# A one-core attention-and-MLP block on Trainium2: all engine queues in a newly found order, and a narrower marking product

## The chip, the core and the metric

The kernel runs on one core of one Trainium2 chip, in one launch. The core has five engines with a queue of instructions each: TensorE (PE; its weight loads are listed as PEld), VectorE (DVE), ScalarE (ACT), GpSimd (POOL) and SyncE (SP), whose queue here holds nearly all DMAs. 16 DMA engines move the data. The metric is the device time of one execution in microseconds (us).

## The reference

Two blocks on a sequence of 2048 tokens of width 512, in bf16. The first is linear attention with 32 heads of width 16, the second a gated MLP whose gate mixes the tokens with a 2048 x 2048 matrix.

```python
# A: x = A_x, 2048 x 512
q, k, v = heads(layernorm(x) @ wqkv)
phi = lambda t: where(t > 0, t + 1, exp(t)) + 1e-06
kv  = einsum('bhsd,bhse->bhde', phi(k), v)
z   = sum over tokens of phi(k)
o   = (phi(q) @ kv) / (phi(q) . z + 1e-06)
h   = x + o @ wo
# B
y   = gelu(layernorm(h) @ w_in)              # 2048 x 1792
z1, z2 = y[:, :896], layernorm(y[:, 896:])
g   = w_sp @ z2 + b_sp                       # tokens mixed, 2048 x 2048
out = h + (z1 * g) @ w_out
```

## The kernel before

**How it is recorded.** The kernel function records operations with an engine, a function that emits the instructions, the memory it reads and writes, and a cost (`_Prog.add`). Dependences follow from the memory. `schedule` takes the order of all operations from a packed string, `ORDER`; each engine's queue is that order cut down to the engine. `emit` writes the queues and puts a semaphore wait wherever a queue needs something of another engine or of a DMA. So the string decides what stands behind what on each engine, and nothing else of the order is decided at run time: an engine that waits holds up all that is queued behind it.

**Lines.** Every group of matrix products made by `matmuls` carries L434, every activation L453, plain DMAs L464 (`dma`), DMA transposes L467 (`dma_t`), and the sums and differences of `comb` L755. L815 are the DMAs that spread the reciprocals of the attention's denominators over the partitions (r, from rcp). L692 is the accumulation of the keys' outer products over the tokens.

**Stages.** Tokens are taken in 16 tiles of 128 (n = 0 to 15).

- Head: x arrives in pieces of one or two tiles. `k_unit(n)` handles the tiles n and n + 1: row statistics (VectorE, L543), reciprocal deviation (ScalarE or GpSimd), the normalized rows xn, their transpose xnT, the key product with wqkv, phi (L614, L619) into pk, and the accumulation L692. The first four tiles are transposed by TensorE (L602), all later ones by a DMA transpose on SyncE's queue:

```python
            if n < HEAD:                                        # HEAD = 4
                pe_transposes(xn[:, i, :], b + i % 2, xnT, i, second)
            else:
                g.last = dma_t(xnT[:, :, i * P:(i + 1) * P], xn[:, i, :], f"xt{i}")
```

- `q_unit` makes two 128-column chunks of the queries for 512 tokens; two units of the first 512 tokens stand among the first key tiles. Their weights are the DMA called wq.
- The loads of the weights that are needed later, w_v (a part of wqkv), wo, four halves of w_in (win1, win2) and the transposed blocks of w_sp (wt0 to wt15, two DMA transposes each), are recorded without a wait on any compute engine; that they follow the last load of x is the only order asked for. Where among the transposes of xnT they are issued is a matter of `ORDER`.
- Attention out: the value path (L790), denominators (L824), phi(q) times the reciprocals (L840), products with m, residual rows h (L852), and their normalized rows hn, transposed by DMA into hnT.
- MLP: Strassen-like cells (`cell3`, `cell2`, L882) form y with sums and differences of quarters of w_in (ws) and of hnT (hs); `mix` does the same for the product with w_sp, partly nested once more (`nested`, L1051), and applies the gate (L1030, L1031).
- Out: each gated tile z1 is transposed by DMA into zgT; `mo_pair` computes two output tiles from seven products in two PSUM banks X and Y (6 and 7, for the last pair 3 and 4), and `mo` the last two tiles. [...]

Of the kernel before, what the change touches and what calls it, by code (L numbers as in the profile page):

```python
# [32 lines left out]
class _Prog:  # L33
# [219 lines left out]
def bass_sequential_preLN__linear_attn_block__mixer_gmlp__prompt_kernel(  # L253
# [24 lines left out]
    g = _Prog(nc)  # L278
# [43 lines left out]
    x = g.sbuf("x", o_x, [NT, D], BF16)  # L322
    h = g.sbuf("h", o_x, [NT, D], BF16)
# [6 lines left out]
    hnT = g.sbuf("hnT", o_pk, [KD, S], BF16)  # L330
# [4 lines left out]
    z1 = [g.sbuf(f"z1t{n}", o_xnT + slot[n] * ZR, [FH], BF16) for n in range(NT)]  # L335
# [14 lines left out]
    N4 = HT // 2 * (HW // 2) * 2  # L350
# [65 lines left out]
    def bank(b, n=512, lo=0):  # L416
        return psum[:, b, lo:lo + n]
# [5 lines left out]
    def PE(fn, reads, writes, ns, **k):  # L423
        return g.add("PE", fn, reads, writes, cost=ns, lat=165, **k)
# [372 lines left out]
    for c in range(KD):  # L797
        b = CB[1 - c % 2]
# [18 lines left out]
    for tg in range(NG):  # L817
# [12 lines left out]
        if tg not in MERGE:  # L830
# [135 lines left out]
    lo, hi = slice(0, HW), slice(HW, FH)  # L966
# [227 lines left out]
    for k in range(0, HT, 2):  # L1194
# [5 lines left out]
        if k == 0:  # L1200
# [9 lines left out]
    PE(lambda pe: pe.matmul(bank(7), lhsT=hnT[:, 0, 0:P], rhs=wout[:, 0, :], start=True, stop=True), [hnT[:, 0, 0:P], wout[:, 0, :]],  # L1210
       [bank(7)], 216)
    wout_sums()
    for c, i in enumerate(MIX[:-1]):
        X, Y = (3, 4) if i == MIX[-2] else (6, 7)
        if Y != 7:
            rest, any_, w = psum[:, Y, HW:512], zgT[MIX[0]][:, 0, :], wout[:, 0, 0:512 - HW]
            PE(lambda pe, rest=rest, any_=any_, w=w: pe.matmul(rest, lhsT=any_, rhs=w, start=False, stop=True,
                                                               skip_group_check=True), [any_, w], [rest], 65)
        mo_pair(i, c % 2, X, Y)
# [34 lines left out]
```

## Time and profile before

| | |
|---|---|
| time, median of 3 runs | 224.73 us (223.61 to 225.98) |
| span of the profiled execution, first to last instruction | 222.3 us |
| the profiled execution's own time | not listed beside its span |
| busy: PE, DVE, ACT, POOL | 216.2, 202.8, 142.8, 47.1 us |
| matrix products and weight loads | 1346 each |
| granted TensorE clock | 1.000 |
| DMA | 27.12 MB, 57% of the 16 engines' time on SyncE's queue |

In the profile, a row of the timeline reads: start, duration (both us), engine, line, operation, output <- inputs, count; in square brackets the idle time before it and what ended it. A row of the windows reads: stretch, length, then busy time and number of instructions of PE, PEld, DVE, ACT and POOL, the granted clock, the share of the 16 DMA engines and GB/s. A row of the DMA view reads: what, queue, operation, count, size of one, median us from issue to landing. A row of the waits reads: engine, what it works on, line, what it waited for, total us, times, longest. "SPq" is SyncE's DMA queue.

### The profile page before, as it was taken

To read this page: it belongs to the slowest core of one execution; us is meant where nothing else is said; L and a number is where in the kernel's file an instruction comes from. 1 tells how busy PE (TensorE), PEld (TensorE's weight loads), DVE (VectorE), ACT (ScalarE), POOL (GpSimd) and SP (SyncE) were. 2 spreads that over 40 slices of the span, in tenths; PEclk is the share of its full clock that TensorE was granted. 3 is DMA by queue.
4 is the path that set the end of the run, shared out by engine and by line. 5 is a ranking of instruction groups with operands and counts; after the bars stand their busy time and mean duration, and the time that the engine had idled before them with its cause. 6 is when DMAs were issued, how large, how long until landed. Compare 5 with 4: busy or idle time off the path is not lost.

```text
span 222.3 us, 3865 instructions
## 1 busy us (share of the span) xinstructions
PE 216.2 (97%) x1346; PEld 123.6 (56%) x1346; DVE 202.8 (91%) x472; ACT 142.8 (64%) x283; POOL 47.1 (21%) x133
## 2 busy tenths in 40 slices
PE   7799999999999999999999999999999999999995
PEld 7443444443344444444555556666676787767764
DVE  3899967899999999999989998999999989899995
ACT  5789663299889999999872546626475246732330
POOL 4334410000547554685720000000000000000000
PEclk9999999999999999999999999999999999999999
DMA  6758877928966555304993653995372205033574
GB/s 182 246 99 227 170 180 181 237 50 193 182 137 132 112 107 85 49 0 94 179 134 88 166 116 81 161 202 107 58 152 58 41 0 70 17 88 27 127 203 142
DMA packets 75026, 27.12 MB, mean 122 GB/s; under 512 B 64768, under 2 KB 75008, under 8 KB 75008
## 3 DMA queue, kind: packets, MB, share of 16 engines
q1 hardware_dynamic: 74304, 26.30, 57.0%
q10 hardware_dynamic: 704, 0.59, 0.9%
q8 instruction: 10, 0.16, 0.3%
q14 instruction: 8, 0.07, 0.1%
HBM read 6.95 MB, written 2.10 MB: 41 GB/s over the span
## 4 chain that ended last, share of the span: by engine, by line
PE 87%; DVE 4%; DMA 3%; ACT 3%; SPq 1%; issue 1%; ACTq 0%
PE psum L434 79%; PE psum L692 6%; DMA x<-in_A_x_dram 1%; SPq L815 1%; DMA r<-rcp 1%; ACT e L453 1%; DVE pqT L840 1%; DVE h L852 1%; DVE st L543 1%; DVE pk L619 1%; PE psum L602 0%; PE psum L824 0%; PE psum L714 0%; PE psum L790 0%; DVE e L614 0%
## 5 line engine op out<-in xcount | busy, mean ns | idle before, releaser
L453 ACT ACTIVATE psum<-psum 128x448 f32<-128x448 f32 (+2 forms) x76 | 31.1, 428 | 34.9 <-PE psum L434 28.6
L434 PE MATMUL psum<-z,wt 128*128 128x448 bf16 (+1 forms) x216 | 42.0, 335 | 0.1
L434 PEld LDWEIGHTS psum<-z,wt 128*128 128x128 bf16 x216 | 20.9, 98 | 14.6 <-ACT np L453 0.4
L434 PE MATMUL psum<-win,hnT 128*128 128x448 bf16 x112 | 26.4, 353 | 0.0
L453 ACT ACTIVATE e<-psum 128x1024 bf16<-128x1024 f32 (+1 forms) x18 | 16.7, 929 | 8.5 <-PE psum L434 8.5
L453 ACT ACTIVATE z1t<-psum 128x448 bf16<-128x448 f32 (+1 forms) x24 | 16.4, 691 | 7.3 <-PE psum L434 5.3
L434 PE MATMUL psum<-ws,hs 128*128 128x448 bf16 x72 | 19.2, 353 | 0.0
L434 PEld LDWEIGHTS psum<-win,hnT 128*128 128x128 bf16 x112 | 10.5, 98 | 11.0 <-ACT z1t L453 1.0
L434 PE MATMUL psum<-zt,sa 128*128 128x448 bf16 (+1 forms) x92 | 16.5, 316 | 0.0
L882 DVE TENSOR_TENSOR psum<-psum,p5z 128x448 f32<-128x448 f32 x24 | 15.0, 626 | 1.0 <-ACT z1t L453 0.8
L692 PE MATMUL psum<-pk,xn 128*128 128x512 bf16 x64 | 15.8, 379 | 0.1
L453 ACT ACTIVATE p<-psum,b 128x448 f32<-128x448 f32 x22 | 13.4, 634 | 3.6 <-DVE u L1030 1.8
L434 PE MATMUL psum<-m,pqT 128*128 128x512 bf16 x64 | 14.7, 380 | 0.9 <-DVE h L852 0.6
L434 PE MATMUL psum<-xnT,wqkv 128*128 128x512 bf16 x64 | 15.3, 379 | 0.0
L453 ACT ACTIVATE z<-psum 128x896 bf16<-128x896 f32 x16 | 15.0, 970 | 0.2 <-PE psum L434 0.2
L434 PE MATMUL psum<-wqkv,xnT 128*128 128x512 bf16 x64 | 15.0, 379 | 0.0
L1030 DVE TENSOR_TENSOR u<-psum,p 128x448 bf16<-128x448 f32 x22 | 13.6, 620 | 1.4 <-PE psum L434 1.0
L434 PE MATMUL psum<-wout,zgT 128*128 128x256 bf16 (+1 forms) x77 | 14.9, 302 | 0.0
L434 PE MATMUL psum<-nv,nu 128*128 128x224 bf16 x108 | 14.5, 259 | 0.1
L543 DVE BATCH_NORM_STATS2 st<-x 128x6 f32<-128x512 bf16 x15 | 9.8, 682 | 3.6 <-DMA x<-in_A_x_dram 3.6
L614 DVE TENSOR_SCALAR e<-e 128x1024 bf16<-128x1024 bf16 (+1 forms) x18 | 7.0, 390 | 5.6 <-ACT e L453 5.6
L434 PEld LDWEIGHTS psum<-zt,sa 128*128 128x128 bf16 x92 | 8.9, 98 | 5.3
(157 smaller groups left out, 452.2 us busy)
## 6 DMA issues: line engine op xcount, KB each, us to landing
r<-rcp SPq DMA_DIRECT2D x16, 128.0 KB, 2.7
out_dram<-h SPq DMA_DIRECT2D x15, 128.0 KB, 1.8
win<-in_B_w_in_dram SPq DMA_DIRECT2D x4, 448.0 KB, 3.8
x<-in_A_x_dram SPq DMA_DIRECT2D x6, 256.0 KB, 3.8
wqkv<-in_A_wqkv_dram SPq DMA_DIRECT2D x2, 512.0 KB, 4.9
wout<-in_B_w_out_dram SPq DMA_DIRECT2D x1, 896.0 KB, 5.1
wt<-in_B_w_sp_dram SPq DMA_TRANSPOSE x32, 4.1
wo<-in_A_wo_dram SPq DMA_DIRECT2D x1, 512.0 KB, 6.4
```

Source lines behind the costliest of these rows:

```text
L434: inst = pe.matmul(out_ap, lhsT=a, rhs=b, start=start and i == 0, stop=stop and i == len(pairs) - 1, **kw)
L453: return g.add("ACT", lambda ac: ac.activation(out_ap, in_ap, func, **kw), [in_ap, *extra], [out_ap] + ([accum] if accum is not None else []),
L543: dve(lambda v: v.bn_stats(s[:, 0:6], src[:, n, :]), [src[:, n, :]], [s[:, 0:6]], D)
L614: dve(lambda v: v.tensor_scalar(e, e, 1.0, EPS_PHI, op0=ALU.min, op1=ALU.add), [e], [e], w * GW, acc=4)
L619: dve(lambda v: v.scalar_tensor_tensor(dst, t, 1.0 + EPS_PHI, e, op0=ALU.add, op1=ALU.max), [t, e], [dst], w * GW, ps=True)
L692: inst = pe.matmul(bank(CB[c]), lhsT=xn[:, i, c * P:(c + 1) * P], rhs=pk[:, i, :], start=i == 0, stop=i == NT - 1)
L815: g.add("SP", lambda q: q.dma_start(dst, src_ap), [rcp[:, i:i + w, :]], [dst], cost=700, lat=2200, dma=f"r{tg}{c // 2}")
L840: dve(lambda v, q=q, r=r: v.tensor_tensor(q, q, r, ALU.mult), [q, r], [q], 2 * GW, acc=2)
L852: dve(lambda v, n=n, b=b, s=s: v.scalar_tensor_tensor(h[:, n, :], bank(b), 1.0, x[:, n, :], op0=ALU.mult, op1=ALU.add, accum_out=s[:, 0:1] ...
L882: dve(lambda v: v.tensor_tensor(half(b), half(src), p, ALU.add), [half(src), p], [half(b)], HW, ps=True)
L1030: dve(lambda v: v.tensor_tensor(u, half(b), p, ALU.add), [half(b), p], [u], HW, ps=True)
```

## The change

The order string is another one, found by a new search over the same operations, and the product that marks bank 7 is made 64 columns wide, by the code that marked the last pair's bank:

```diff
-ORDER = "c-jrsg92EG76ibvyXVHXZM%(a+qN4!jcwbuZQHgR+kEdQX3Qd3M1#e%kQT`z..."
+ORDER = "c-jTQ0{|EY5Cp)zz5Up>8{4+i#<p#{v28WBZQHhO+v!Y101;q_2S*4Hkr4?(..."
...
-    PE(lambda pe: pe.matmul(bank(7), lhsT=hnT[:, 0, 0:P], rhs=wout[:, 0, :], start=True, stop=True), [hnT[:, 0, 0:P], wout[:, 0, :]],
-       [bank(7)], 216)
     wout_sums()
     for c, i in enumerate(MIX[:-1]):
         X, Y = (3, 4) if i == MIX[-2] else (6, 7)
-        if Y != 7:
+        if c == 0 or Y != 7:
             rest, any_, w = psum[:, Y, HW:512], zgT[MIX[0]][:, 0, :], wout[:, 0, 0:512 - HW]
             PE(lambda pe, rest=rest, any_=any_, w=w: pe.matmul(rest, lhsT=any_, rhs=w, start=False, stop=True,
                                                                skip_group_check=True), [any_, w], [rest], 65)
```

All five queues are in another order; the numbers of operations are the same (349 on TensorE, 456 on VectorE, 255 on ScalarE, 129 on GpSimd, 126 on SyncE). The first operations of SyncE's queue, before and after, with tiles in parentheses:

```
     before                            after
 1-4 x(0), x(2), wk, x(4,5)            the same
 5-8 x(6,7), x(8,9), wq, x(10,11)      the same
 9   xnT(5)                            x(12,13)
10   xnT(4)                            x(14,15)
11   x(12,13)                          wt10, second half
12   xnT(6)                            win2, first half
13   xnT(7)                            win2, second half
14   x(14,15)                          win1, one half
15   win2, first half                  wo
16   xnT(9)                            xnT(4)
17   xnT(8)                            xnT(5)
18   xnT(11)                           win1, other half
19   xnT(10)                           xnT(7)
20   win1, one half                    xnT(6)
21   xnT(12)                           xnT(9)
22   xnT(13)                           xnT(8)
...
33   wt10, one half                    wt0, one of ten wt blocks in a row
34   r (first of 16)                   wt11
43   r                                 r (first of 16)
```

TensorE's first twelve groups of four products after the transposes (K: key product of a tile; A: accumulation of a tile; Q: query product):

```
before  K0 K3 K1 K2 A0 Q Q Q A1 Q A2 K5
after   K0 K1 K2 K3 Q Q A0 Q Q A1 K4 K5
```

The accumulations A2 and A3 follow K5 in the changed order, then the key products of tiles 7 and 6. On VectorE the differences of w_in's quarters (ws) start seven places earlier, and more row statistics stand ahead of the normalization of tiles 4 and 5. The last products, the last additions and the last stores keep their order but for neighbours that change places.

More of the change, by code (lines that the diff above doesn't have):

```diff
@@ L15 @@
 SEM_NS = 45.0
-ORDER = "c-jrsg92EG76ibvyXVHXZM%(a+qN4!jcwbuZQHgR+kEdQX3Qd3M1#e%kQT`zTPO=_AuOClv8Wc>qFG!EZ()okbBk|*C9&w1z;at6OK3?grzN&zmdA2gDobv8EuW>f6jsPmS{lo5g)OZWup*Yu3R(=yVCgNU)v;n0%Q9Il%VHU=u4T5`*4FA-QLArREt|ErzpS`5vg}sU8e1D{XF05bwYPt)ft9urR?!+-U+Z8Ut&^3ps#ePSS!}Che_LlOYhA3rRkmvOuT`-D*3|}DIje3HZLl@9I5x<J*?7BQO>Brwvf)<4CRj}?Z<DQ=O|hXi&AM50n`$j=x^=giw#Zsq51VC6td%Xb#n#hi*fJYwy==LSuoZU8R@y4tWxZ{Wjk49Y+xA)?+h=QRwC%UqHpbT40Xt}iY>qv#n>N<w+F@H~M{J(WxAk_^#@PnjiUqdOHrY12ZCmY;J-3Cn-5%R9+hIHHxLvdBw%JbDe|FBE*-1NVr)-Ozw@bDS7wm<dw##<k&e#=uYCCb!Lg15qw2-)JpY4@>u$Xvfp+LN}SO7vJ3}WMp3Gt8!@$uCnBQfH@5g;ypSQ31*DEMwE@Y7NwIieyV{#a7{vT!g&M>0f1SUj)<_-!$e2Dy<6X;Bt=5FQzj5=D>>c@Y8WQ32%;5&4i2`B4-FP#*Uz5(=UYilHL1pg0PlKI$SX3Zn!{A~RYe8%iM)D&cRmLj%;qU#N^WsDhqoh#aVjYAB5@$d2}Cgg&T_GU$cjXpDc*7i}>LwU7(7(E*2%6JOB;M=$~%u?zpA6Q-dlYM?WEV>G&8CTe0oMq)aeVJXI77VcO-%)kot$1)7SYz#zm9K~2HM|XTf3yi}`%)ubs!vTE99lW<5IDxr1hOYR5L%5HY=!U!aiIZ4`*Y*&<&<dxp8jmm@$1wp1@c<KX8bk3IZ|oAD;1vdA9<uW?hG0I<U=3bl0j^*Ya_}mK;WyS|3f^EH{@^b<jc2hP<Tb3vTf`^$H?KoHhpC9mw-zuY6YvHWBPZi=GD7h`B;p2y<~xL7E+*zvB;<K4#506p628YG+(cwPM{agwQbu7KZo~&vR#--5ccx`DF2N>*V>;$xU0y(5_F#TS=VlaSc&6t?^yCY~U?F})ZD!yt6ksprV;z1%M%H5y-bQ^UV^KC>VP;})He@j-XJ+<cITmLGenulkWK8bhOEhMAreG_^;=kO^5{%8(tiUYn%bkqGHXO(=NXd%a#Z=77ww%jK?9Y-M#5gR)*&M)j+|4=c$0i)Y_8iQiT)=ru&G~G~1Kh)5T*%UF#&OKX;cU)D+=2Hj!?#?_@m$5qoWOUyYsdKyS92meup^i716%N+P2vcyVM~7GWPavueBwwRW)&{wT2^H>e&Ifh;uNmqRDS1Zp5QW0<5za#L9XXse&ZOP<PR?A3ZCKyj^!`@<VKd|5pLpdPUj)6<Z13_bwZo@hi7>1|Mc#~3{stWlr<;?a^2^7hR_y<)Ha@FD0Sg6&SYp^WIEkr6@^hvhSeor;8xycI9=v7hSw}U;uTicRX$)Ob!7xS=0ir*9$aT+)#43C(Gx~fRNdr%jIO7wqpFIfTa2M+yv>-Zr8|tRnu?>i+Q)h-sCatLgo>}6ddURJr9{fB#LB0nN}?C6uU9OpWGbeHdd&t(uHt&bluDu8YNQfMrIJdoLQ11js;wf*q|$1v!b+|3%C9CWqY65q?5e9uYN`Tip|V=4f0R)zl}ByVUagf?9aK)u)LE0&T$xovUDQ!iv|Jg~Nz>KVE2^t{sG7QIn!2l%dTN0F)=IVWHJYJp8mND~zxrvWX6d`;Xtidmx7KQ|)~THasjYr!yf$dC)@!5s=!k}>msaVh7HX(QsDp3PFm2W%4Od?s)>ci`NS)Nb+M;Eer)?Ug(ORN|`b+bbR^j}VCTN$&=(iT=tj21wj%%DIYP$|;w|1zL?^O=%R7XFppW3HCdaN_bqU##zdlcT!>4yH(Bpp*EKd)4NNf&feceFy6wO<!?Kv(tT|7G72{H}f}vR~12MfENo-DCPa(L1}my}wX2cfY2mx~*9LQh~?u2;S9WdmF#6DBjIOcz5sN!#%Et^amQ@J$=6S@)#b<M|p3L=lQ*lztX?n*ZX^X590$pu@CZop2QRQ0w3V1J)w{GAwI^3`Wub)<UZcVc`^^}6aAqkcqxCRbUw+`dm_){lf9}Z^(p>LQ$3@<)oV@nus+Rac?zH5GrfS%@wvX;7y4p<r$xTR)A)NW^_0Hcmw5*Ntd;&jJAH+x^~}D?cX%d0?`yr9XYtj3!6SMO&*|$utFQ4*UfTciY@Xe7d39gs1%0D$@W1_|F8Xf&q%FS3w|XJZ>wA5$@Aopk&$sz5Kj?-1fS2_zI^>r;pFi`XUe1quO+V#_{iN6OuR7wFy|$P4V_wH|`w6e$SG<PT^D}<d>v|C{=JoxB7xk<D+^_j{Z|uXoxZm^!-o#6K3BTbDy`nesTi)Coc?<uh+kV$8`5nLSoBf_w_A1`gANfOn;30yR{@7pnYiBUqTm3)skiiq5=W&AnJXD~dwZHK&LFnL}hYQ~NX%8C&!3Pf?y!3Pa-aUvE#0{SMM~@Ih3E~A2gD)OE_~y}qPyWLr2Qh-r9yR#s@q?JbFOL;`^#noe;JYUZ{&>RRw<iuPND}-H1t^N4"
@@ new lines @@
+ORDER = "c-jTQ0{|EY5Cp)zz5Up>8{4+i#<p#{v28WBZQHhO+v!Y101;q_2S*4Hkr4?(fT)OqxQK@MNP=95j-*I{JV=N{NQT@<jJ)^@`H&LHksqm$0)>$pF;D<SkOnbP5JgcNX%P$QQ4{G98->sc84w2<Q42e*4Kkw`G9fG4A`6P64z8m$N+28RA|$fo2I`>{%Ht+Vq73??9j>7Q+T(B3M?>U519U)XghEIBgNmqverSX)sD!Hc7yVHg1CSH9Fc8(y730wuq0tG|5e5@55lt`{oiPZ*5EhFO4rS34lTZVbF&yPE1w+sb-7yu-F%;7<9o;Y!3o!#N&;yIG1iP^mEwK!bF$+C063fvG;qeG7FaoRb6#roq_FyO0pf`45C7xg}_F*)(SRahRe$2)JtinNz#T*>MI2^`YJjXgb#5}CU3mm}~tjBy@#RhD}M%=~%Y{MQqitRXt9oTN0a2$7V7F+EEHsd7j;|$(mo1MZroW=v3$3<MgCw#yT3u&Km2_F%{F5@n);2C1tON27oJ;bumW){X`+ZVXSvsXxD@l6)lz9O;3wZMKLiN&#Rh+^N7+<xL0{<5f+$`aZigtKG@i*89RnuWCl_8X}!hUKyFmePt^UQ1*DSOm*w8LXH^wDOkU(pw5EU}deKrL)>r+zMGFOKat<gcY{TR?;e15i4c&EQ^)4I@ZdvS|+P#Ijp|5wYpZxGFo=4Y@6+nwYDmj(|TG}YiHT4nl-RK*2@mtaI0zUt*_OxHa5!2SZ@2*I@nkH+d5h<>uuHTnDw&}HqH854eMm1ZKTb#&eqVT+ZgL&OKhLbutqk^j#y(`YRj#O{bvL0fDN=|_RaQNQ(Iw2?YND#@7CS!+Bj=rw{5l^w3XJ<=GaebW^?U?-LdiZ!|vI8tg;?9$X?@t{j!s`+8)|{n`h1Kl&!Hhcw}qsqII=(_Sjz8Q0r!wEE^}-X`64a?XnHF?3`#<?6(cEw-9sija@Zzk`1%B7N3hOC#RV6k6p8=7BDVDG6BI{G{$2nKC#7?h}Z3%-LTL+W4W1_A^6lLTS7jwjds?;FbUt=O^eJAmYR8(l$-3MMPWCdv-K91QJIF_xxk|FmWAU&E5zrPm**`ld$5uh;3tdDI^1CC*pvDB!t${o`>+-ZbFal<QPyP<re|&TVlgJ;1*^~E?91N#i!oW24VawuSc3mD1sgIJGjKa&^QARnIfmypMqo*1WE@6hOMbTU%)}jR#evMsNSwn8Y|SrLiYd91ZCILF*q>!sk%Raj2e2)7aW?yLE{Cuk=d&?~avt|F6$f)Sn{XHxuqnr}J^$u#X5~WevbXHOMSRbW9M6^9&q{2@34F(6tjrHw#VVZ0s_ewYY|at<$VvRn)tt;v9LYmm!@XR>Q5?-F{KBam!xsF?<6O#rIE~-Amfv`Q%lL!KxsJcMp4E7m8~B?mxRD1roj<vWe>j%rn+ZS5t)w4eb#~@Go?|tiLHE-PTz-^ic!DAP4nz8RUSL`e?Ohql?{W*n_)LcNaNdO%8Qu%|Dc0ag)?@^~#D~1fh<=%~c%N4o$*=JdBl~q$@!B56A2XUq^#{DcCyee-S<@?f43FhCJf=V6O~&?Hyv?{C$DgyV$Mb~#g7H0<zhnZ>>iIm8=l8_EhXp;UC-K}~%wMsdC-dU|n)UrJZ{VHuh9$g%Qh0LD;|;x}r}R>u!Bcx-FYUFwsHgKrUdD@fIZx#U{BLjU<^8zV@r?eDH}Q(T#G8A2&+F;EthexX-r6g8Ca>;Iy@R*%$==L6`&8d;Exn7c@V1`AtNLp1=xe=)cT`u;=H0xt*83FS;5~i1Z}K*p;cdLXck)@@PTjqqukiu?-E;af@8!eQ+q3vUAE8m2>EnH{ANK#ej}P)8KF$035&zd$`fOk7BYci$_n|(_H~Ime>%)DEkMw!Iz|;6D-|U(FgpcyAzR*YeQD5voe7+y^Q@+l(`62)52YtIw@G*YU$NCQ6>EnE&FY>lJ?aTd)k5oAA_Ot%m!|R-1^j&`5JL`|{^$Y&kFZmvy<kvis_W5Oh<WKy%N0ABI@6i=ixBZGg_ZuEfH=T;9ryfhG)kV*|y<B&^t6q3F#Zh<l&|UAPm)=wNe4ctMf?`Yh<ptD7|0<>WDo_md*L;OgTrE^T4N^S4@&OvC*B)P?6jGx#RAV$mi4|I7b=AWti4y3Rk5^v3@q|jIM2f7xG*S0`oRTV)Cg_2ORa(9EhdxQ^G*$0>x~gchX6e1}&=f6D1|`>L&!w4~rqcT0GqgyvwOA1~M+LP+DYR7ElwQlULff@mUp$jm>YOrar`G7BXVxmE(I;Q0^IEMe+Mw*(sH|G6Y+A1z+NI6ftt~2}+}fkPDx`~grkvWR!pf)o`di=pfQo3p{?T(C)K{;n>N=vbI;3MdtQtC@nmVbYDyLdHrQ<59+Pb9EDz7?vsk%C&%etU?s;1)Fsw>K)s~W6p+N4G*p&Kfu>uRi0DyjOapr&e|v%0BfYN+PArHZ<v+q$PFs;pspAPes5q5e~dpoLy(u3oF9?u)?_g$xwL2`VX6@K_$a(Nl#E!UU}pE_kc3!8?6W5QGoj>xCXEZV)N>s0hIq#S0<^-xMYIsmMXJAZqYQ(S!KG4}DgQAXX4F_^Mw@5PVmn;ExgpzZE-393V&%{12myilG"
```

## The prediction

> **What bounds the kernel now.** I read the page of the profiled execution first, for the busy shares, and then its windows stretch by stretch.
>
> ```profile
> span 222.3 us, 3865 instructions
> ...
> PE 216.2 (97%) x1346; PEld 123.6 (56%) x1346; DVE 202.8 (91%) x472; ACT 142.8 (64%) x283; POOL 47.1 (21%) x133
> ```
>
> ```profile
> 7.96:16.59 8.63, 8.63 (x43) 3.85 (x41) 8.00 (x24) 7.05 (x12) 2.67 (x8) 1.00 0.67 156
> 16.59:23.95 7.36, 7.24 (x33) 2.95 (x32) 6.98 (x14) 5.95 (x7) 2.70 (x8) 1.00 0.92 217
> 23.95:45.90 21.95, 21.95 (x117) 9.48 (x115) 17.25 (x28) 10.85 (x15) 2.90 (x8) 1.00 0.83 191
> 45.90:54.40 8.50, 8.37 (x57) 3.78 (x57) 8.04 (x14) 8.13 (x12) 0.00 (x0) 1.00 0.45 103
> 54.40:67.70 13.30, 12.46 (x59) 5.06 (x60) 12.44 (x33) 11.56 (x26) 6.24 (x21) 1.00 0.77 158
> 67.70:171.90 104.20, 103.98 (x615) 58.08 (x616) 101.06 (x232) 75.06 (x156) 28.81 (x70) 1.00 0.59 110
> 171.90:219.50 47.60, 47.60 (x370) 35.21 (x367) 44.27 (x123) 19.75 (x50) 0.00 (x0) 1.00 0.35 76
> ```
>
> A row gives the stretch, its length, the busy time of TensorE, its weight loads, VectorE, ScalarE and GpSimd, the granted clock, the share of the 16 DMA engines and GB/s. TensorE is the bound from 7.96 us to 219.5 us at full clock. Its idle time is 0.12 us in the second stretch, 0.13, 0.84 and 0.22 us in the fourth to the sixth, and none in the others: 1.3 us in all. (A product's record is 379 ns and its slot 216 ns, as four take 0.86 us below, so a wait under 0.16 us doesn't show here; with some ten such waits the truth may be near 3 us.) So reordering can win little, and a wait that an order adds on TensorE before 219 us goes into the time nearly whole.
>
> The head is where the orders differ most, so I read the timeline of TensorE there, and that of SyncE's DMA queue.
>
> ```profile
> 7.96 3.62 PE L434 MATMUL psum<-wqkv,xnT 128*128 128x512 bf16 x16
> 11.41 1.03 PE L692 MATMUL psum<-pk,xn 128*128 128x512 bf16 x4
> 12.28 2.75 PE L434 MATMUL psum<-xnT,wqkv 128*128 128x512 bf16 x12
> 14.87 1.03 PE L692 MATMUL psum<-pk,xn 128*128 128x512 bf16 x4
> 15.73 1.03 PE L434 MATMUL psum<-xnT,wqkv 128*128 128x512 bf16 x4
> 16.59 1.03 PE L692 MATMUL psum<-pk,xn 128*128 128x512 bf16 x4
> 17.46 1.89 PE L434 MATMUL psum<-wqkv,xnT 128*128 128x512 bf16 x8
> ```
>
> ```profile
> 7.52 0.47 SPq L464 DMA_DIRECT2D wqkv<-in_A_wqkv_dram  x1
> 8.04 0.51 SPq L464 DMA_DIRECT2D x<-in_A_x_dram  x1
> 11.88 3.27 SPq L467 DMA_TRANSPOSE xnT<-xn  x2
> 15.20 0.58 SPq L464 DMA_DIRECT2D x<-in_A_x_dram  x1
> ```
>
> From 7.96 to 16.59 us TensorE does ten groups of four products of 0.863 us each on the first four token tiles. The group at 17.46 us is the first on tiles 4 and 5, whose normalized rows come through the DMA transposes issued at 11.88 and 13.2 us. SyncE issues them with nothing new queued in between after the load at 8.04 us.
>
> **The change, the wide product.** The marking product is taken out and a narrow one put in.
>
> ```profile
> 176.12 0.21 PE psum L1210
> ...
> 212.07 0.03 PE psum L1217
> ```
>
> In the chain that ended last the 512-column product is worth 0.21 us, the existing 64-column one 0.03 us. I take 0.18 us gained. It can't be more than 0.21; below, it is nothing if TensorE waits there for the transposed gate tile, which the products beside it read as well.
>
> **The change, the early SyncE queue.** After the load that stands at 8.04 us, the changed order issues, before the first transpose: the last two loads of x (256 KB each), half of a transposed block of w_sp (256 KB), three of the four loads of w_in (448 KB each) and w_o (512 KB). Before, only the transposes followed. By issue time alone this costs nothing: six loads of 0.47 to 0.58 us and one weight transpose, 1.39 us in the row below, end near 13.2 us, and VectorE now normalizes tiles 4 and 5 later too (its queue has more row statistics ahead of them, so near 13.5 us). The price is in the data. How the queue lands what it is given is seen where the kernel before puts two loads ahead of a transpose (issue times from the timeline, times to landing from the DMA views of the stretches around each issue):
>
> ```profile
> 37.22 0.58 SPq L464 DMA_DIRECT2D wqkv<-in_A_wqkv_dram  x1
> 37.84 0.51 SPq L464 DMA_DIRECT2D wo<-in_A_wo_dram  x1
> 38.39 5.60 SPq L467 DMA_TRANSPOSE wt<-in_B_w_sp_dram  x2
> ...
> 53.77 1.39 SPq L467 DMA_TRANSPOSE wt<-in_B_w_sp_dram  x1
> ```
>
> ```profile
> wqkv<-in_A_wqkv_dram SPq DMA_DIRECT2D x1, 512.0 KB, 5.2
> wo<-in_A_wo_dram SPq DMA_DIRECT2D x1, 512.0 KB, 6.4
> ```
>
> ```profile
> wt<-in_B_w_sp_dram SPq DMA_TRANSPOSE x1, 6.7
> ```
>
> Landings are 42.4, 44.2 and, for the transpose issued at 38.39, 45.1 us: in the order of issue, 1.8 us apart for 512 KB (284 KB per us), and 0.9 us for the transposed 256 KB. With little ahead of them transposes of xnT need half as long:
>
> ```profile
> xnT<-xn SPq DMA_TRANSPOSE x12, 3.2
> ```
>
> So the transpose of tile 4 will land behind everything issued earlier. The queue's state at the point where the orders part is known:
>
> ```profile
> wqkv<-in_A_wqkv_dram SPq DMA_DIRECT2D x1, 512.0 KB, 4.6
> x<-in_A_x_dram SPq DMA_DIRECT2D x1, 256.0 KB, 4.7
> ```
>
> These are the issues at 7.52 and 8.04 us; they land at 12.1 and 12.7 us. Ahead of tile 4 there are then 2 x 256 + 256 + 3 x 448 + 512 = 2624 KB. At 284 KB per us that is 9.2 us; with 0.45 us for its own 128 KB (half of 0.9) it lands at 12.7 + 9.2 + 0.45 = 22.4 us. The bounds are the fastest and a slow stretch of the DMA engines here:
>
> ```profile
> 40.00:42.00 2.00, 2.00 (x19) 0.79 (x21) 1.29 (x3) 1.13 (x2) 0.00 (x0) 1.00 1.01 352
> ```
>
> 352 GB/s (344 KB per us) gives 7.6 us and a landing at 20.8 us; the 217 GB/s at a share of 0.92 in the stretch 16.59:23.95 is 230 KB per us at a full share, 11.4 us and 24.6 us. I take 22.4, since its rate comes from loads of these very shapes with a backlog. [...]
>
> In the changed order TensorE's first ten groups are the same ten as before in another sequence; the eleventh and twelfth are tiles 4 and 5, ahead of the two accumulations that stood at 16.59 and 19.18 us. TensorE reaches the query products at 11.4 us and waits 0.7 us for their weights (landing 12.1), so it stands before tile 4 at 17.3 us, in order, with everything else queued behind it, and stays there until 22.45 us. Against 16.59 us that is **+5.9 us** (4.2 to 8.0). The queue behind follows: tile 5 lands 0.45 us after tile 4; one more w_in load (1.6 us) and two transposes bring tiles 6 and 7 to near 25.4 us, and TensorE wants them after four groups, at 25.9 us.
>
> **What comes back.** (a) The eight groups from 16.59 us take 7.36 us before but only 8 x 0.863 = 6.91 us of work; their waits were for a tile's exponent and product, which the four groups between now cover: -0.45 us. (b) VectorE and the loads are ahead by then: w_in is there early, and the differences of its quarters stand earlier in VectorE's queue.
>
> ```profile
> L755 DVE TENSOR_TENSOR ws<-win 128x896 bf16<-128x896 bf16 x4 | 2.4, 608 | 0.0
> ```
>
> Four of these, and those made from them, can run in the hole. In front of the first residual row VectorE has the same instructions in both orders, and 5 us more time for them. Of the 1.2 us idle from 45.9 to 171.9 us I take 0.9 as won back; the ends are 2.2 (all, with short waits that the records hide) and 0, since these waits are loops from TensorE over ScalarE, DMA and VectorE back to TensorE, and such a loop keeps its length wherever it starts. (c) The product, -0.18. Later queues are rearranged locally, gate and weight transposes by a few places; I cost them at nothing, since TensorE waits for no DMA but those of the head:
>
> ```profile
> PEld psum L434 <- DMA xnT<-xn: 0.6, 2, 0.4
> ...
> PEld psum L434 <- DMA wqkv<-in_A_wqkv_dram: 0.2, 1, 0.2
> ```
>
> What hides the later ones is that they land ahead of their use; if that cover is gone, one such place costs up to a landing, 3 to 4 us. The tail (last stores, last products) keeps its order.
>
> Sum: 5.9 - 0.45 - 0.9 - 0.18 = **+4.4 us**. The span is 222.3, so 226.7; around the span lie about 2.4 us (median 224.73 less span, as the profiled execution's own time isn't shown beside it), which gives **229.1 us**. With the ends: 4.2 - 0.45 - 2.2 - 0.2 = +1.4 (226.1) and 8.0 - 0.45 = +7.5 (232.2).
>
> **Rivals.** *Transposes get past the loads* (not slower): the queue spreads each DMA over 16 engines, and if a transpose lands as its 3.2 us says (issue near 13.5, landing near 17), TensorE waits 0.7 us for the query weights and nothing more. Then 222.3 + 0.7 - 0.45 - 0.9 - 0.18 = 221.5, time 223.9. It decides as soon as tile 4 lands before 17.4 us. For it: the transpose issued right behind a w_in load near 19.5 us took only 3.8 us.
>
> ```profile
> xnT<-xn SPq DMA_TRANSPOSE x1, 3.8
> ```
>
> Against: wo and the weight transposes at 6.4 and 6.7 us. [...]
>
> *The wait is there, but most is given back*: fast DMA (+4.2) and all of the later idle time, 226.1 to 226.6 us. For it: 1.3 us of visible idle; against: no idle at all from 23.95 to 45.9 and from 171.9 on.
>
> *SyncE itself is held up*: two weight transposes behind 1 MB took 5.60 us to issue, not 2.8. If tile 4's issue ends only as w_o lands (21.5 us), tile 5 follows 1.25 us later and lands near 24.8 (+1.4), and ten weight transposes at 1.39 us, which now stand ahead of the r round, reach it 1 to 2 us late: 4.4 + 1.4 + 1.2 = +7.0 us, 231.7.
>
> **How the numbers follow.** Forecast (wait of about 6 us, little returned) 0.70; overtaking 0.10; mostly returned 0.10; queue held up 0.10. The range 225.8 to 232.0 holds the forecast's bounds and most of the second and third; outside lie the first and some of the last, under 0.2. A measurement of this kernel tells about 1% (222.5 to 227.0) from no change. Faster by over 1% needs overtaking and more idle time won than the records show: 0.04. Within 1%: the rest of the first and two thirds of the second, 0.13. Slower: 0.83.
>
> **What would show it.** In the profile after: TensorE idle for about 5 us from 17.3 us, released by the DMA of xnT; the longest landing of xnT near 9 us; DMA share near 1 from 12 to 22 us; the following stages like before, about 4 to 5 us late; the last products 5 us later with the same tail. If xnT lands within 4 us and TensorE doesn't stop at tile 4, the mechanism is wrong; if it stops for 5 us and the time still rises by under 2 us, the term that failed is what comes back.

## The result, and the profile after

The changed kernel takes 235.22 us (median of 4 runs, 233.22 to 235.58) against 224.7 us: a ratio of 1.046, 95% interval 1.040 to 1.052. It is slower, as forecast, but by 10.5 us where 4.4 were forecast, and beyond the range of 225.8 to 232.0. The profiled execution took 235.17 us with a span of 233.4, 11.1 us more than before.

The page of the kernel after, and its windows over the stretches that the prediction showed of before:

```profile
span 233.4 us, 3850 instructions
...
PE 218.3 (94%) x1333; PEld 123.5 (53%) x1346; DVE 203.7 (87%) x472; ACT 143.0 (61%) x283; POOL 50.9 (22%) x133
...
PEclk9999799999999999999999999999999999999999
```

```profile
7.96:16.59 8.63, 7.72 (x36) 3.36 (x36) 8.30 (x24) 6.01 (x10) 3.31 (x10) 1.00 0.95 264
16.59:23.95 7.36, 1.78 (x7) 0.57 (x6) 4.12 (x8) 2.46 (x3) 3.69 (x11) 0.91 1.23 289
23.95:45.90 21.95, 21.84 (x96) 9.70 (x97) 14.55 (x24) 11.66 (x14) 3.50 (x9) 0.95 0.57 125
45.90:54.40 8.50, 8.45 (x54) 3.32 (x52) 6.24 (x10) 4.72 (x8) 0.00 (x0) 1.00 1.05 169
54.40:67.70 13.30, 11.58 (x69) 5.13 (x68) 11.51 (x22) 11.18 (x19) 1.47 (x3) 1.00 0.88 185
67.70:180.90 113.20, 111.51 (x645) 60.15 (x646) 108.89 (x253) 81.76 (x171) 36.25 (x87) 1.00 0.48 93
180.90:230.50 49.60, 48.71 (x371) 35.48 (x374) 45.82 (x123) 20.44 (x51) 0.00 (x0) 1.00 0.35 72
```

From 16.59 to 23.95 us TensorE was busy for 7.24 us before and for 1.78 us now. The granted clock, 1.00 in every stretch before, is 0.91 and 0.95 in two stretches here. And idle time stands where there was hardly any: 1.7 us in the stretch from 54.4, 1.7 in the next and 0.9 in the last, against 0.84, 0.22 and 0.00 in the corresponding stretches before. (The last two stretches end 9 and 11 us later than those of before, to hold about the same work.)

TensorE's timeline of the kernel after:

```profile
12.27 1.89 PE L434 MATMUL psum<-xnT,wqkv 128*128 128x512 bf16 x8 [0.83 <-DMA wqkv<-in_A_wqkv_dram]
...
23.18 3.31 PE L434 MATMUL psum<-wqkv,xnT 128*128 128x512 bf16 x8 [5.58 <-DMA xnT<-xn]
26.32 1.89 PE L692 MATMUL psum<-pk,xn 128*128 128x512 bf16 x7
...
63.44 4.48 PE L434 MATMUL psum<-m,pqT 128*128 128x512 bf16 x20 [1.56 <-ACT e L453]
...
150.16 0.56 PE L434 MATMUL psum<-z,wt 128*128 128x224 bf16 x4 [0.54 <-ACT z1t L453]
...
222.95 0.50 PE L434 MATMUL psum<-vs,us 128*128 128x256 bf16 x3 [0.58 <-DVE us L755]
```

The first two rows are the head as forecast: the wait for the query weights, then the stop at tile 4. The last three are waits of the later stages. The row at 23.18 holds one more thing: its eight products take 3.31 us, where eight such products take 1.89 us at 12.27.

To see where the time is lost I compared the kernels at equal work: I added up the slots of TensorE's products in queue order (0.216 us for 512 columns, less in proportion: 0.190 for 448, as eight of those take 1.68 us at 173.35 us of the kernel before, with a record of 0.352 us) and noted by how much later than before each kernel starts the product at which the sum has reached a given value. (Some of these traces lack the records of 12 or 13 products; they are counted in at their weight loads, which are all there. The products that e5 adds are left out.) The times in the first column are those of the kernel before; of the seven kernels behind "after" each is described at its experiment.

```
 before   after  e2     e3     e5     e6     e7     e9     e10
  16.2    +0.7   +0.1   +0.3   +0.5   +0.6   +0.3   +0.6   +0.2
  26.5    +7.5   +5.8   +2.0   +5.3   +6.9   +1.6   +2.1   +0.6
  51.6    +7.6   +8.5   +2.0   +5.4   +6.9   +1.7   +2.2   +0.6
  57.2    +9.0   +8.9   +7.0   +6.7   +6.9   +1.7   +2.2   +0.6
  88.4    +8.9  +10.2   +5.9   +7.0   +7.1   +1.6   +2.0   -0.1
 137.0    +9.1  +10.1   +6.1   +7.7   +7.3   +1.8   +2.0    0.0
 143.6    +9.9  +10.5   +6.7   +8.3   +8.4   +2.6   +2.0   +1.1
 161.6   +10.3  +10.5   +6.6   +9.3   +8.3   +2.7   +2.0   +1.0
 209.7   +10.4  +15.4   +6.6   +9.5   +8.3   +2.9   +1.8   +0.9
 216.0   +11.0  +15.6   +7.1   +9.6   +8.4   +3.7   +1.8   +1.3
```

Column "after" has three steps: 7.5 us in the head, 1.5 us near 57 us (the products that need phi(q) times r), and 1.9 us from 137 us on. No step leads back.

### The profile page after: what moved, and what is told of

Read it like the earlier page. It is cut to its first block, busy times and chain, and to the rows that moved or that the text cites. A ratio compares the mean times of both kernels' runs of the same rounds, so it can differ in the third digit from the quotient of the medians.

```text
span 233.4 us, 3850 instructions
## 1 busy us (share of the span) xinstructions
PE 218.3 (94%) x1333; PEld 123.5 (53%) x1346; DVE 203.7 (87%) x472; ACT 143.0 (61%) x283; POOL 50.9 (22%) x133
## 4 chain that ended last, share of the span: by engine, by line
PE 68%; DVE 15%; DMA 12%; POOL 1%; issue 1%; ACT 1%; SPq 1%; DVEq 0%
PE psum L434 61%; PE psum L692 5%; DMA zgT<-z1t 5%; DMA xnT<-xn 4%; DMA x<-in_A_x_dram 3%; DVE nv L755 2%; DVE u L1030 2%; DVE pqT L840 1%; DMA r<-rcp 1%; DVE st L543 1%; DVE nu L755 1%; DVE h L1188 1%; DVE h L852 1%; SPq L464 1%; DVE wt L755 1%
## 5 line engine op out<-in xcount | busy, mean ns | idle before, releaser
L453 ACT ACTIVATE psum<-psum 128x224 f32<-128x224 f32 (+2 forms) x76 | 31.3, 425 | 34.6 <-PE psum L434 27.1
L434 PE MATMUL psum<-wqkv,xnT 128*128 128x512 bf16 x63 | 16.2, 405 | 5.7 <-DMA xnT<-xn 5.6
L434 PE MATMUL psum<-ws,hs 128*128 128x448 bf16 x72 | 18.7, 353 | 0.0
L453 ACT ACTIVATE p<-psum,b 128x448 f32<-128x448 f32 x22 | 13.4, 633 | 5.6 <-PE psum L434 2.3
L434 PEld LDWEIGHTS psum<-win,hnT 128*128 128x128 bf16 x112 | 10.6, 98 | 10.9 <-ACT z L453 0.9
L434 PEld LDWEIGHTS psum<-wqkv,xnT 128*128 128x128 bf16 x64 | 6.4, 103 | 14.1 <-issue 7.7
L567 POOL TENSOR_SCALAR st<-st 128x1 f32<-128x1 f32 x10 | 4.8, 481 | 37.6 <-ACT sh L453 33.0
```

Source lines behind the costliest of these rows:

```text
L434: inst = pe.matmul(out_ap, lhsT=a, rhs=b, start=start and i == 0, stop=stop and i == len(pairs) - 1, **kw)
L453: return g.add("ACT", lambda ac: ac.activation(out_ap, in_ap, func, **kw), [in_ap, *extra], [out_ap] + ([accum] if accum is not None else []),
L567: pool(lambda p: p.tensor_scalar(s[:, 2:3], s[:, 0:1], s[:, 0:1], -1.0 / (n * n), op0=ALU.mult, op1=ALU.mult), [s[:, 0:1]], [s[:, 2:3]], 240)
```

## The experiments

Two theories stood against each other. **The queue**: the loss comes from the order of SyncE's queue, by the backlog of loads ahead of xnT, by the slow clock behind the wait, and by the weight transposes ahead of the r round. **The orders**: the changed orders of the other engines cost a good part by themselves. The kernels differ in queue orders alone, except for e4 and e5 and for the narrow product, which e2 and e10 have too. The runs of one kernel differ by 0.5 to 4.3 us here, so a difference of 1 to 3 us between two kernels is read together with the traces.

**e1 and e2: the queue alone, one way and the other.** e1 is the kernel after with SyncE's queue of before. e2 is the kernel before with SyncE's queue of after:

```diff
 e1:  TensorE, VectorE, ScalarE, GpSimd: as after
-     SyncE: as after
+     SyncE: as before
 e2:  TensorE, VectorE, ScalarE, GpSimd: as before
-     SyncE: as before
+     SyncE: as after
```

> The changed kernel with one queue exchanged: SyncE issues its DMAs in the order of the kernel before; TensorE, VectorE, ScalarE and GpSimd keep the changed orders, the product stays narrow. Theory Q (the loss of 10.5 us comes from SyncE's queue alone: the backlog in front of xnT, the slower clock behind the wait, the weight transposes ahead of r): 223 to 226 us, xnT landing within 4 us, no wait of TensorE over 1 us. Theory O (the other engines' orders cost a good part too): 228 us or more with the xnT wait gone.

> The kernel before with only SyncE's queue in the changed order (all other engines in the order of before; the product narrow). Theory Q: 233 to 237 us, TensorE idle about 5 to 6 us in front of the first tile that comes through a DMA transpose. Theory O: 229 to 231 us, the rest of the loss being the other engines'.

e1 took 254.91 us (ratio 1.134, 1.126 to 1.142), and its waits for xnT were not gone (three, 3.2 us in all). e2 took 240.55 us (1.076, 1.069 to 1.082), above the ranges of both theories. Both are slower than either kernel, which neither theory expected. Rows of TensorE's timeline, of e1 and then of e2:

```profile
40.77 1.89 PE L692 MATMUL psum<-pk,xn 128*128 128x512 bf16 x4 [8.07 <-DVE pk L619]
```

```profile
22.10 1.92 PE L434 MATMUL psum<-wqkv,xnT 128*128 128x512 bf16 x6 [4.40 <-DMA xnT<-xn]
...
38.77 1.67 PE L434 MATMUL psum<-wqkv,xnT 128*128 128x512 bf16 x7 [2.73 <-DMA xnT<-xn]
```

e2 shows that the queue of after is enough for a stop at tile 4 (4.40 us) whatever the other engines do. Beyond that these two runs settle little: a queue taken from one kernel meets engines that make and want the tiles in another sequence (5 before 4 and 6 before 7 in the one, 4 before 5 and 7 before 6 in the other), and new waits of 2.7 to 8 us appear, most likely from that mismatch. The later experiments therefore move single entries within one kernel.

**e3: the loads behind the transposes.** The kernel after with six entries of SyncE's queue moved, nothing else:

```diff
-  wt10b, win2a, win2b, win1a, wo, xnT4, xnT5, win1b, xnT7, xnT6, xnT9, xnT8, ...
+  xnT4, xnT5, win2a, xnT7, xnT6, win2b, xnT9, xnT8, win1a, ... win1b, ... wo, wv, wt10b
```

> The changed kernel with six DMAs of SyncE's head moved behind transposes of xnT: the four halves of w_in one by one behind the transposes of tiles 5, 6, 8 and 11, wo behind tile 15, the half of wt10 behind the value weights. The ten weight transposes in front of the r round stay. Theory Q: the head's wait and the slow clock go (7.5 us), the late r round stays or shrinks: 226 to 229 us, TensorE at tile 4 by 17.5 us, granted clock 1.000. If the loads were not what xnT waits for, the time stays at 234 to 236.

It took 232.34 us (1.038, 1.032 to 1.044), 2.9 us less than the kernel after, but more than the 226 to 229 us expected. TensorE's timeline and the waits of e3:

```profile
25.09 1.90 PE L434 MATMUL psum<-wqkv,xnT 128*128 128x512 bf16 x8 [0.56 <-DMA xnT<-xn]
27.71 1.02 PE L434 MATMUL psum<-wqkv,xnT 128*128 128x512 bf16 x4 [0.72 <-DMA xnT<-xn]
...
60.02 5.82 PE L434 MATMUL psum<-m,pqT 128*128 128x512 bf16 x20 [3.67 <-DVE pqT L840]
```

```profile
DVE pqT L840 <- DMA r<-rcp: 3.8, 1, 3.8
```

```profile
36.91 16.97 SPq L467 DMA_TRANSPOSE wt<-in_B_w_sp_dram  x11
53.93 7.84 SPq L815 DMA_DIRECT2D r<-rcp  x12
```

The stop at tile 4 is gone, and the lateness of the head falls from 7.5 to 2.0 us. But 5 us of it reappear at 57 us: the weight transposes keep SyncE busy until 53.9 us (last fence, SyncE's timeline), the r copies start only then, and VectorE waits 3.8 us for them. In the kernel after the same transposes delay r by only 1.5 us, since there everything, the reciprocals too, comes 5.5 us later out of the head. The wait at 60 us is 3.67 us and the 20 products behind it take 5.82 us instead of 4.48: 1.3 us more.

**e4: the narrow product alone.** The kernel before, with the marking product of bank 7 (L1210, 512 columns) at 64 columns, the width of the last pair's (L1217); no run was without these products:

```diff
-    PE(lambda pe: pe.matmul(bank(7), lhsT=hnT[:, 0, 0:P], rhs=wout[:, 0, :], start=True, stop=True), ...
...
-        if Y != 7:
+        if c == 0 or Y != 7:
```

> The kernel before, all queues in its own order, only the marking product 64 columns wide. Theory: 0 to 0.2 us gained, 224.5 to 224.7, not told from no change. If the narrow product waited for something new, a stall at its place in the last third and over 225.

223.76 us, ratio 0.9997 (0.997 to 1.0025): no difference that can be told, and the 0.18 us priced lie inside the interval.

**e5: the wait filled.** The kernel after with 24 more products behind the accumulation of tile 1; their weights are zeros, so that they add nothing to banks 4 to 7:

```diff
+            for c in range(24 if i == 1 else 0):
+                inst = pe.matmul(bank(CB[c % KD]), lhsT=warm, rhs=pk[:, i, :], start=False, stop=False)
```

> The changed kernel with 24 added products of 512 columns on TensorE (zero weights, accumulated onto banks 4 to 7 right behind the accumulation of tile 1, so they add zero; about 5.2 us at 216 ns each), nothing else changed. They fill the wait for tile 4's xnT, so TensorE works through it without the values being any different. Theory that the slowed clock behind the wait costs its share: the granted clock stays at 1.00 from 22 to 28 us, the first eight products after the wait take 1.9 us instead of 3.31, and the time falls 1.2 to 1.4 us below that of the changed kernel, to about 233.9. Rival, that this lost time is made up later anyway, or that the clock falls for another reason: the same 235.2 within 0.5. If the fill overshoots the wait, tile 4 starts up to 0.5 us later than in the changed kernel.

233.63 us (1.040, 1.035 to 1.045), 1.6 us below the kernel after. The windows of the kernel after, then those of e5, and e5's timeline:

```profile
22.00:24.00 2.00, 0.82 (x3) 0.29 (x4) 0.00 (x0) 0.00 (x0) 0.00 (x0) 0.67 0.96 266
24.00:26.00 2.00, 2.00 (x6) 0.72 (x5) 0.00 (x0) 0.00 (x0) 0.00 (x0) 0.50 0.98 227
26.00:28.00 2.00, 1.95 (x9) 0.88 (x9) 0.42 (x1) 1.48 (x2) 0.00 (x0) 0.98 0.00 0
```

```profile
22.00:24.00 2.00, 2.00 (x11) 0.93 (x10) 0.00 (x0) 0.00 (x0) 0.00 (x0) 1.00 1.15 317
24.00:26.00 2.00, 2.00 (x11) 0.91 (x10) 0.56 (x2) 1.65 (x3) 0.00 (x0) 1.00 0.36 78
```

```profile
17.24 5.34 PE L695 MATMUL psum<-pk,warm 128*128 128x512 bf16 x23
22.42 1.89 PE L434 MATMUL psum<-wqkv,xnT 128*128 128x512 bf16 x8
```

With TensorE kept busy the clock stays at 1.00 and the eight products take 1.89 us again. The kernel after ran them at a granted clock of 0.50, for some 3 us behind the wait. So 1.4 us of the head's loss (3.31 less 1.89) is not waiting but slow work behind the wait. The rest of the gain in the table's row at 26.5 us (2.2 in all) is a start at 22.42 instead of 23.18 us, in a part that the edit does not touch. Not all of it lasts: at 216.0 us e5 is 1.4 us ahead of the kernel after. The runs of e5 (231.52 to 233.91 us) overlap those of the kernel after (233.22 to 235.58), so the size of the clock's share rests on the traces.

**e6: weight transposes behind the r round.** The kernel after with five of the ten wt transposes that stand ahead of r moved behind the last transpose of hnT.

```diff
-  wt x10, r, ..., hnT (last)
+  wt x5, r, ..., hnT (last), wt x5
```

> The changed kernel with five of the ten weight transposes that stand ahead of the r round in SyncE's queue moved behind the last hnT transpose, nothing else. Theory that they hold up the r round: SyncE issues the first r copy when rcp is ready (55.8 us, not 57.2), VectorE's wait for r of 1.6 us goes, and the time falls about 1.5 us, to 233.7. Rival, that VectorE and ScalarE are what is late there: 235.2, no change within 0.5.

232.66 us (1.036, 1.033 to 1.039), 2.6 us below the kernel after. SyncE's and VectorE's timelines of the kernel after, then SyncE's and TensorE's of e6:

```profile
41.98 15.19 SPq L467 DMA_TRANSPOSE wt<-in_B_w_sp_dram  x10
57.22 9.15 SPq L815 DMA_DIRECT2D r<-rcp  x12
```

```profile
61.07 0.69 DVE L840 TENSOR_TENSOR pqT<-pqT,r 128x1024 bf16<-128x1024 bf16 x1 [1.58 <-DMA r<-rcp]
```

```profile
40.84 8.39 SPq L467 DMA_TRANSPOSE wt<-in_B_w_sp_dram  x5
55.15 10.55 SPq L815 DMA_DIRECT2D r<-rcp  x12
```

```profile
61.30 4.48 PE L434 MATMUL psum<-m,pqT 128*128 128x512 bf16 x20
```

The ten transposes end at 57.17 us and hold the r copies back; with five, SyncE is free from 49.2 us, the r copies start when rcp is ready, and the products follow without a wait. The profile puts the wait at 63.44 us of the kernel after down to ScalarE's e, the last of what those products need; that r is what makes it late is shown by e6, where it goes with the moved transposes alone. The step of 1.5 us near 57 us is gone from the table. Another 0.7 us of the gain is a head that came out of its wait earlier in this run, in a part that the edit does not touch.

**e7 and e8: both moves, and the loads one place later.** e7 is e3 and e6 together; e8 is e7 with each of the four w_in loads two transposes further back.

```diff
 e8 against e7:
-  xnT4, xnT5, win2a, xnT7, xnT6, win2b, xnT9, xnT8, win1a, ...
+  xnT4, xnT5, xnT7, xnT6, win2a, xnT9, xnT8, win2b, xnT10, xnT11, win1a, ...
```

> Both moves: six early loads behind the xnT transposes (as in the run where the loads are spread) and five weight transposes behind the last hnT transpose. Theory that the two queue faults are all of the loss up to 80 us: the 4.5 us at the r round that the spread loads brought out go, the wait of pqT for r falls below 0.5 us, and the time is 227.5 to 228.5. Rival, that the other engines' orders cost a good part: not below 230.

> As the run before, with the spread loads one place later each (the first half of win behind xnT of tile 6, the second behind 8, win for the second operand behind 10 and 13, wo behind 15), so that tiles 4 and 5 have nothing in front of them but the four first loads. Theory: the xnT waits of 0.6 and 0.7 us near 25 and 28 us go as well, 225 to 227. If a later load is then late for its first use, a new wait on win appears before 45 us and the time stays near 228.

e7 took 228.01 us (1.016, 1.014 to 1.019): as the theory of the queue had it, 7.2 us below the kernel after from eleven moved DMAs. e8 took 229.78 us (1.024, 1.022 to 1.026), a miss. In e8's profile TensorE waits 2.35 us for the query weights ahead of tile 4, though the queue up to there is the same in both; the DMA views around that load, of e7 and then of e8:

```profile
wqkv<-in_A_wqkv_dram SPq DMA_DIRECT2D x1, 512.0 KB, 3.9
```

```profile
wqkv<-in_A_wqkv_dram SPq DMA_DIRECT2D x1, 512.0 KB, 5.8
```

The same transfer landed 1.9 us later, and the cause stays open; the four runs of e8 lie within 0.5 us of each other, so its loss is no accident of the profiled one. e8 also kept the waits for xnT near 26 and 29 us (0.49 and 0.76 us). They are the waits for tiles 9 and 10, and in e8 as in e7 one w_in load stands right ahead of each of these tiles. So e8 does not tell whether the loads cause them.

**e9 and e10: the two halves of the orders.** e9 is e7 in which every engine takes the orders of the kernel before for all operations that start after 108.5 us in the kernel after. e10 is the complement: the orders of before up to there, those of after behind.

```diff
 e9:   up to 108.5 us: as e7
-      from there: all engines as after
+      from there: all engines as before
 e10:  up to 108.5 us: as before
-      from there: all engines as before
+      from there: all engines as after
```

> The kernel with both queue moves (early loads behind the xnT transposes, five weight transposes behind the last hnT transpose), and in it every engine takes the orders of the kernel before for all operations that start after 108.5 us in the changed kernel. Theory that the orders of the second half cost their own part: the 0.8 us near 140 us and the 0.8 us at the end go, the lateness stays near 1.6 us from 28 us on, and the time is 226.1 to 226.5. Rival, that these two follow from the first half (from how late each engine comes out of it): 228.0, no change within 0.5.

> The complement: the orders of the kernel before for all operations that start before 108.5 us in the changed kernel, the changed orders from there on, narrow marking product. Theory that the second half costs its own part: 1.4 to 1.9 us above the kernel before, 225.6 to 226.1. Rival, that the second half only passes on what it is given: 224.2 within 0.5.

e9 took 226.57 us (1.012, 1.008 to 1.015), e10 225.50 us (1.007, 1.005 to 1.010): each 0.1 us outside the theory's range and far from its rival's. In e9 the lateness stays near 2.0 us from 57 us to the end, and the waits that e7 has near 143 and 216 us are gone; e10 comes to the second half on time and loses 1.1 us near 143 us and 0.4 us at the end. Rows of e7's timeline, then of e10's:

```profile
142.84 0.56 PE L434 MATMUL psum<-z,wt 128*128 128x224 bf16 x4 [0.54 <-ACT z1t L453]
...
215.70 0.50 PE L434 MATMUL psum<-vs,us 128*128 128x256 bf16 x3 [0.82 <-DVE us L755]
```

```profile
141.33 0.56 PE L434 MATMUL psum<-z,wt 128*128 128x224 bf16 x4 [0.77 <-ACT z1t L453]
...
213.25 0.50 PE L434 MATMUL psum<-vs,us 128*128 128x256 bf16 x3 [0.34 <-DVE us L755]
```

These two waits belong to the orders of the second half: they come with these orders on a punctual first half too. The halves add up: e9 is 2.5 us above before and e10 1.4, e7 3.8.

**e11: tiles normalized earlier.** e9 with VectorE's normalization of tiles 4 and 5 ahead of a row statistic and two small operations, and ScalarE's of tile 6 ahead of an exponent.

```diff
 VectorE:
-  phi (L619), e, statistics, e, xn4, xn5, ...
+  phi (L619), xn4, xn5, e, e, ..., statistics
 ScalarE:
-  e (query chunk 1), xn7, e (query chunk 2), xn6
+  e (query chunk 1), xn7, xn6, e (query chunk 2)
```

> The kernel of the run where the second half has the orders of before, and in its head VectorE normalizes tiles 4 and 5 right behind the second product of phi of tile 0's neighbour, ahead of one row statistics and two smaller operations, and ScalarE normalizes tile 6 ahead of the exponent of the second query chunk. Theory that what is left of the head's loss comes from VectorE's and ScalarE's orders, which start SyncE's transposes at 13.6 us instead of 11.9: the first transpose is issued near 12.6 us, the waits of TensorE for xnT near 25 and 27 us (0.3 and 0.76 us) shrink to 0.2 us together, and the time is 0.8 us below that run. Rival, that SyncE's queue alone is late by its load order: no change within 0.4.

226.31 us (1.010, 1.007 to 1.013), 0.3 us below e9: the rival's number, but not a test of its reason, as the step meant was not reached. In its profile the query weights landed 1.25 us later than in e9, the first transpose was issued at 13.4 us, not 12.6, and the profile puts TensorE's longest wait in the head, 1.66 us, down to ScalarE's e. The last 2 us, which e9 still loses in the head, are explained in part. In e9's profile TensorE waits 0.74 us for the query weights, whose products stand one place earlier than before, and 1.40 us in three waits for xnT. What makes xnT late there stays open: that VectorE's order starts the transposes late (13.7 us, before 11.9) was only argued, and the w_in loads between the transposes were not taken away.

No version beat the kernel before.

## Why the prediction was right or wrong

The direction and the mechanism of the head were right: TensorE stops at tile 4 because its transpose stands behind 2624 KB of loads, and a wait there is not given back. The sum was wrong in four terms: the slow clock behind the wait, the idle time won back, the transposes ahead of r, and the orders of the second half. Term by term, with the table's numbers:

| term | forecast | measured |
|---|---|---|
| tile 4's products start (16.59 us before) | 22.45 (+5.9) | 23.18 (+6.6) |
| slow clock behind the wait | not priced | +1.4 |
| (a) short waits of the first tiles, covered now | -0.45 | -0.45 |
| (b) idle time won back from 45.9 to 171.9 us | -0.9 | 0 |
| (c) narrow product | -0.18 | none seen (e4: -0.7 to +0.6) |
| weight transposes ahead of r | 0 (third rival: +1 to 2) | +1.5 |
| orders of the second half | 0 | +1.9 |
| sum | +4.4 | +10.9 (span: +11.1) |

Outside the sum, around the span lie 1.8 us (235.17 less 233.4) where 2.4 were taken; with 1.8 the same sum would have given 228.5 us instead of 229.1.

**The landing.** The rate was right. Rows of the DMA views, the last load of x that stood in the queue before too and w_o, and one of the chain that ended last:

```profile
x<-in_A_x_dram SPq DMA_DIRECT2D x1, 256.0 KB, 5.1
...
wo<-in_A_wo_dram SPq DMA_DIRECT2D x1, 512.0 KB, 8.7
```

```profile
14.55 8.50 DMA xnT<-xn
```

Issued at 8.63 and 13.90 us, the two loads landed at 13.7 and 22.6: 2624 KB in 8.9 us, 295 KB per us, where 284 was taken. The transpose, issued at 14.55 us, landed at 23.05, 0.45 us behind w_o, just as taken. The 0.65 us by which the landing was missed came in ahead of the backlog: that load of x was issued 0.6 us later than before and landed 1.0 us later. The rival of overtaking fell, since the transpose landed behind w_o. Its premise, that a DMA is spread over the 16 engines, is seen in the kernel before: the load of w_out, with nothing else under way, took a share of 1.08 of them from 122 to 123 us, at 386 GB/s, and the transposes of xnT alone 0.85 from 13.2 to 13.3 us. But the landings here kept the order of issue (13.7, 22.6 and 23.05 us), so the order was the thing to price by, as the forecast did.

**The clock.** The step that failed first: the products behind the wait were priced at the full clock. The trace of before has no stretch below 1.00, but it has no wait of this length either (TensorE's longest is 1.0 us, at the start), so it could not show what a long wait does. The price needed an upper end for that, and no number of before gives one. The kernel after shows a clock of 0.50 from 24 to 26 us and of 1.00 again from 28 us on. That cost 1.4 us here, and 1.7 in e6 (eight groups from 22.25 to 30.84 us, 8.59 us for 6.91 us of work). In e1 and e2 the shorter waits of 2.77 and 3.15 us were followed by 0.50 too.

**What comes back.** (a) held: the eight groups behind the wait run without a gap, from 23.18 to 31.50 us, and 6.6 + 1.4 - 0.45 makes the 7.5 us of the table. (b) is the step that failed outright: of the 0.9 us nothing came. The lateness of 7.5 us stands unchanged from 26.5 to 51.6 us and only grows behind that; in e6, without the step at r, it goes from 6.9 to 7.3 us between 26.5 and 137.0 us, so r does not hide a gain. The prediction had named this end: the idle places are loops through TensorE itself, which keep their length. That this is the reason was not tested.

**The r round.** The third rival was right about this place: the weight transposes reached r late, and it cost 1.5 us where 1 to 2 were named. It was given 0.10 as one rival together with a later tile 5 (which landed 0.5 us behind tile 4 and cost nothing). But the moved transposes needed no rival: ten issues of 1.39 us ahead of r stood in the list of the change, and belonged into the sum.

**The second half.** "I cost them at nothing, since TensorE waits for no DMA but those of the head" was wrong by 1.9 us. The waits are shown as waits for ScalarE's z1t and VectorE's us; behind us stands the landing of the last gate transposes. The chain that ended last and VectorE's timeline of the kernel after:

```profile
219.63 2.89 DMA zgT<-z1t
```

```profile
222.54 0.36 DVE L755 TENSOR_TENSOR us<-zgT 128x384 bf16<-128x384 bf16 x1 [0.35 <-DMA zgT<-z1t]
```

The transpose lands at 222.52 us, the sum starts at 222.54, and TensorE goes on at 222.95. A wait list that names no DMA for TensorE says only that the DMAs were in time in that order.

## What to carry to other kernels

When a load is moved ahead of a transfer that the bound engine waits for, add up the bytes ahead and divide by the rate at which that queue lands such loads; here this gave the landing within 0.65 us. The long waits on TensorE cost more than their length here: 1.4 us more behind the one of 5.58 us, 1.3 us behind that of 3.67 us in e3. A transfer that looks in time may be so only because something ahead of it is late: e3 took 5.5 us out of the head and got 2.9. Where every queue is reordered, price each stage's own new waits; an order with nearly no idle time has nothing to give back and much to lose.

## What the runs showed of the hardware

**Long waits on TensorE were followed by half the clock.** In these runs waits of 1.35 (e5), 1.56 (after), 2.35 (e8) and 2.73 us (e2) left the granted clock at 1.00, and waits of 2.77 (e1), 3.15 (e2), 3.67 (e3), 3.71 (e1), 4.40 (e2), 4.76 (e6), 5.58 (after) and 8.07 us (e1) were followed by a stretch at 0.50. The two outcomes part near 2.75 us here; whether a wait of that length always does the same, these runs do not show. Windows of e2 behind its wait of 2.73 us, of e3 behind that of 3.67 us, and e1's timeline and windows at that of 2.77 us:

```profile
38.00:40.00 2.00, 1.23 (x6) 0.69 (x8) 0.00 (x0) 0.00 (x0) 0.00 (x0) 1.00 0.33 66
```

```profile
60.00:61.00 1.00, 0.97 (x3) 0.42 (x4) 1.00 (x2) 0.00 (x0) 0.00 (x0) 0.50 0.87 190
...
63.00:64.00 1.00, 1.00 (x7) 0.44 (x5) 0.71 (x3) 1.00 (x3) 0.41 (x2) 1.00 0.23 69
```

```profile
216.91 0.64 PE L434 MATMUL psum<-wout,zgT 128*128 128x256 bf16 x3 [2.77 <-DVE h L1188]
```

```profile
216.00:217.00 1.00, 0.09 (x1) 0.10 (x2) 1.00 (x3) 0.00 (x0) 0.00 (x0) 1.00 0.00 0
217.00:218.00 1.00, 1.00 (x7) 0.73 (x7) 1.00 (x3) 0.00 (x0) 0.00 (x0) 0.57 0.00 0
218.00:219.00 1.00, 1.00 (x4) 0.43 (x3) 0.43 (x2) 0.72 (x2) 0.00 (x0) 0.50 0.00 0
```

The clock did not always fall during the wait: in e1 it was still 1.00 when the products started again at 216.91 us.

**The backlog held up the issue too.** Behind the loads one transpose of xnT, that of tile 5, took 3.6 us to issue. The transposes of the kernel after, then of e7, where behind the loads of x never more than one load stands right ahead of one (ns, min/median/max):

```profile
L467 SPq DMA_TRANSPOSE xnT<-xn x12: 1189/1266/3637, 14.5 to 40.0; - x12
```

```profile
L467 SPq DMA_TRANSPOSE xnT<-xn x12: 1188/1264/1335, 13.6 to 34.4; - x12
```
